# The next segment's features made between the matmuls of the last queries, in a segmented-attention and bilinear-GLU block on one core

## The chip, the cores and the metric

The kernel runs on one core of a Trainium2 chip. The core has five engines with a queue each, which run in order: PE (TensorE, matrix products and transposes into the accumulation memory PSUM), ACT (ScalarE), DVE (VectorE), POOL (GpSimd) and SP, which only issues DMAs here (ACT issues some too). The metric is the device time of one execution in microseconds; lower is better. The kernel before takes 881.73 us (median of three runs, 881.40 to 882.42).

## The reference

One transformer block on x of 2048 rows and 512 columns. A vector c gives six modulation vectors (silu(c) @ w_mod). First half: normalise the rows, scale and shift them, and attend with 32 heads of width 16 in four segments of 512 rows:

```python
h = _layernorm(x) * (1 + ca) + sa
q, k, v = h @ wq, h @ wk, h @ wv            # heads of 16, four segments of 512 rows
for s in range(4):
    p = softmax(qs @ ks.T * scale + mask)   # mask adds -1e9 above the diagonal
    a_dot = p @ vs
    pq = phi(qs)                            # phi(t) = t + 1 if t > 0 else exp(t)
    a_mem = (pq @ M) / (pq @ z + 1e-6)      # memory of the segments before
    o = g * a_mem + (1 - g) * a_dot         # g = sigmoid(beta), one per head
    pk = phi(ks)
    M, z = M + pk.T @ vs, z + pk.sum()
x = x + ga * (o @ wo)
```

Second half: normalise again, then ((h @ w_gate) * (h @ w_up)) @ w_down, and add gb times that to x.

## The kernel before

A segment's normalised rows are kept turned around, as *features*: for each 128 of the 512 columns d a tile of 128 x 512 (columns by rows), split in a high part ahH_d (rounded to the fast float32 format) and a low part ahL_d, the rest. A product is then three matmuls per d: high x high, low x high, high x low. The text calls these three matmuls a *triple*.

The attention half is one long loop (the last in the part shown). Its step v handles four heads of one segment (eight steps a segment, 32 in all; a place is written (v, slot)), and has five slots. In each slot PE first runs a **q step** (logits with queries in the rows, whose maximum DVE takes from PSUM: tiles q, nm), then in slot 1 the **tb** products (attention weights times v), then *fill*, and at the end a **k step** (logits with keys in the rows, out of which ACT makes the exponentials, tile pt, and POOL sets the part beyond the diagonal to zero). Each k step needs the exponential of the k step before to have emptied its PSUM tile (lk has one buffer), and a q step needs DVE to be done with the last one.

The **fill** is all the other PE work, in generators that hand out one piece at a time (fill_a, line 955; fill, line 1044). A slot has a credit; a triple costs 0.68 of it, a feature 0.45, a row step nothing. If a generator yields False, the fill of this slot stops there and the credit stays. For each segment s and each group g of eight heads the fill computes kps and qps (a_kq, line 747: k and q of the group, four triples each, over d = 0 to 3), splits them in three bfloat16 parts on ACT and POOL and writes them to DRAM; in the first group also v (vps). Between come the memory steps (mp, up, mz, mT: tiles in the one PSUM buffer sm, emptied by ACT as pkr and us).

The features of the next segment come from ln (line 207) with pfx "a", as a generator a_ln of 13 steps. Nine are *row steps*: four statistics (bn_stats), one for the row scale (ACT and POOL), four that normalise a tile of 128 rows in place (TENSOR_SCALAR x). Four are *feature steps*, one per d: four transposes on PE into a PSUM bank (atp_d), then ACT scales and shifts out of PSUM (ahf, line 205) and rounds to the high part (ahH, line 222), then POOL subtracts for the low part (ahL, line 223). There are eight feature tiles, one set: the next segment's ahH_d goes where this segment's lies, so it can be written only when the last qps (group 3) has read it. The PSUM banks of features, kps, qps and vps are two buffers of tag ms (bank, line 110).

weave(a, b, at) (line 669) hands out a, and after a's i-th piece that costs anything takes as many pieces of b as i stands in at; a False of b is passed on. In the kernel before, lines 977 to 980 weave the nine row steps into groups 2 and 3, and the four feature steps are what is left: they run behind the last qps (line 963), with a False after every second one (line 230).

DVE, ACT and POOL instructions follow the order in which the code and a scheduler put them; row steps are pinned behind the matmul that precedes them in the program.

Of the kernel before, what the change touches and what calls it, by code (L numbers as in the profile page):

```python
# [58 lines left out]
def tile_kernel(ctx, tc, x, wq, wk_, wv, wo, beta, w_gate, w_up, w_down, c, w_mod, out):  # L59
# [147 lines left out]
    def ln(pool, hpool, xt, s, sc, sh, pfx, hb, fast, kept_h=None):  # L207

        first = pfx == "a" and s == 0
        V, A = (CV, CA) if first else (vec, act)  # L210
        yield from ln_rows(pool, xt, s, pfx)
        hH, hL = [], []
        for d in range(KT):
            h = pool.tile([P, L], F32, tag="hf", name=f"{pfx}hf{s}_{d}", bufs=hb[2])
            ln_col(bank(f"{pfx}tp{s}_{d}"), h, xt, d, sc, sh, A)
            hi = hpool.tile([P, L], F32R, tag=hb[0].format(d), name=f"{pfx}hH{s}_{d}", bufs=hb[1])
            lo = hpool.tile([P, L], F32R, tag=hb[0].format(4 + d), name=f"{pfx}hL{s}_{d}", bufs=hb[1])
            if fast:
                V.tensor_copy(hi, h)
                V.tensor_sub(lo, h, hi.bitcast(F32))  # L220
            else:
                act.activation(hi, h, AF.Copy)
                nc.gpsimd.tensor_sub(lo, h, hi.bitcast(F32))  # L223
            hH.append(hi)
            hL.append(lo)
            if kept_h is not None:
                kept_h.append(h)
            yield 0.45
            if not first and d % 2 == 1:
                yield False  # L230
        return hH, hL

# [436 lines left out]
    def weave(a, b, at):  # L669

        i = 0
        for w in a:
            yield w
            if w:
                for _ in range(at.count(i)):
                    w = next(b, None)
                    if w or w is False:
                        yield w
                i += 1
# [275 lines left out]
    def fill_a():  # L955
        for w in w2:
            next(w)
        yield from av
        memq.extend((a_mem(0, 0), a_mem(0, 1)))
        lns = None  # L960
        for s in range(NSEG):
            if s > 0:
                hcur[0] = yield from lns
                if s < 3:
                    r = load_mod(2 * s)
            for g in range(2 if s == 0 else 0, NG):
                ws = []
                if s == 0 and g < 3:
                    ws = [load_g(nm, w, g + 1) for nm, w in (("k", wk_), ("q", wq))]
                for w in ws:  # L970
                    next(w)
                K, Q = a_kq(s, g, "k"), a_kq(s, g, "q")
                if g >= 2 and s + 1 < NSEG:
                    if g == 2:
                        xts[s + 1] = xload(s + 1)
                        lns = a_ln(s + 1)
                        Q = weave(Q, lns, (0, 1, 2, 3) if s > 0 else (2, 3))
                    else:
                        K = weave(K, lns, (0, 2) if s > 0 else (0, 1, 2, 3))
                        Q = weave(Q, lns, (0, 1, 2))  # L980
                if g == 1 and 0 < s < 3:
                    acc = mod_acc(r)
                    K, Q = weave(K, acc, (0, 2)), weave(Q, acc, (0, 2))
                if s == NSEG - 1 and g == 1:
                    xr0 = xr_load(0, pa, (0, 1), "x")
                    ready = chain(wo_weights(), wo_op(0, None, B["orl"], us[0]))
                if s == NSEG - 1 and 0 < g < NG - 1:
                    K, Q = weave(K, ready, (0, 1, 2, 3)), weave(Q, ready, (0, 1, 2, 3))
                if s == NSEG - 1 and g == NG - 1:
                    yield from weave(Q, ready, (0, 1, 2, 3))  # L990
                    memq.append(a_mem(s, g))
                    yield from K
                    yield from ready
                    yield from wo_mm(0, us[0], xr0, (0, 1))
                    break
                yield from K
                for w in ws:
                    next(w)
                yield from Q
                if s > 0 and g == 0:  # L1000
                    while vfree[0] < s:
                        yield None
                    if s < 3:
                        yield from weave(a_v(s), mod_acc(r), (1, 3, 5, 7))
                        yield from a_mod(2 * s, r[0])
                        r = load_mod(2 * s + 1)
                    else:
                        yield from a_v(s)
                        B["orl"] = wo_load(0, wpool)
                if g == 1 and 0 < s < 3:  # L1010
                    yield from a_mod(2 * s + 1, r[0])
                memq.append(a_mem(s, g))
        while memq or memt:
            yield mem_step() or 0.0
            yield False
# [283 lines left out]
    for q in range(2):  # L1299
# [98 lines left out]
        for m in range(2):  # L1398
            s = 2 * q + m
# [111 lines left out]
```

## Time and profile before

| | |
|---|---|
| runs | 882.42, 881.73, 881.40 us |
| the profiled execution | 881.91 us, its span 879.8 us |
| mean granted PE clock | 0.992 |
| PE busy | 832.8 us (95% of the span) |
| DVE, ACT, POOL busy | 650.6, 472.5, 424.1 us |

The profile shows one execution. The timeline has a row for each instruction or run of equal ones: start, length, engine, line, operation, tiles (output<-inputs), size, count, and in brackets how long the engine sat idle before it and what ended that. Most helpers record at line 90 (matmuls), 93 (transposes) or 40 (DVE in the loop), so instructions are told apart by tiles. Matmuls overlap: one of 512 columns is listed with 0.39 us, but the next starts 0.23 us later. The sums by stretch give, for each stretch, its length and then the busy time (and the number of instructions) of PE, PE's weight loads, DVE, ACT and POOL, then the granted PE clock, the busy share of the DMA engines and GB/s; for PE alone they give the length, PE, the clock and the DMA columns. The chain that ended last gives time slices: start, length, what.

### The profile page before, as it was taken

The page shows a single profiled execution, that of the slowest core. Times are in us where ns is not written, and L with a number is a line of the kernel's source. Part 1 is how long each engine was busy: PE and PEld are TensorE (multiplying, and loading weights), DVE is VectorE, ACT ScalarE, POOL GpSimd, SP SyncE. Part 2 cuts the span into 40 slices and gives each one's busy share as a digit, 9 for nine tenths or more (in the row PEclk, how much of TensorE's full clock was granted, in tenths as well). Part 3 has the DMA queues.
Part 4 walks back from the last instruction along what each step waited for, and adds up shares of the span by engine and source line. Part 5 has one row for each costly group of instructions (what it writes and reads, how often), then busy time and mean ns, then how long its engine had stood idle before and what let it go on. Part 6 is the DMA issues. An engine that isn't in the chain of part 4 may idle for free.

```text
span 879.8 us, 14406 instructions
## 1 busy us (share of the span) xinstructions
PE 832.8 (95%) x4824; PEld 583.0 (66%) x4824; DVE 650.6 (74%) x1728; ACT 472.5 (54%) x740; POOL 424.1 (48%) x564
## 2 busy tenths in 40 slices
PE   8998999989999989999978899999999999999998
PEld 5765565555565656655644567788778888887886
DVE  7697677986778868788888759898784856666532
ACT  3757667777677766777554664333363523333321
POOL 4545546546455665486352533987200846550000
PEclk9999899999999999999999999999999999999999
DMA  7774456665648665677695552543414232212032
GB/s 236 225 235 159 146 160 201 214 209 174 207 142 252 199 190 157 220 234 239 209 285 177 160 180 97 176 146 105 163 30 127 87 120 64 56 55 93 0 118 96
DMA packets 112667, 139.46 MB, mean 159 GB/s; under 512 B 20112, under 2 KB 71312, under 8 KB 112592
## 3 DMA queue, kind: packets, MB, share of 16 engines
q1 hardware_dynamic: 106368, 130.91, 48.7%
q10 hardware_dynamic: 6224, 7.62, 2.4%
q8 instruction: 38, 0.62, 0.3%
q14 instruction: 37, 0.30, 0.1%
HBM read 87.48 MB, written 50.76 MB: 157 GB/s over the span
## 4 chain that ended last, share of the span: by engine, by line
PE 66%; DVE 13%; DMA 8%; ACT 5%; POOL 4%; issue 3%; ACTq 1%; SPq 0%; POOLq 0%; DVEq 0%
PE g L90 23%; PE acc L90 14%; PE tb L90 5%; DVE q L40 5%; PE k L90 5%; PE q L90 5%; PE vps L90 4%; PE kps L90 3%; PE qps L90 2%; ACT pt L330 2%; DMA xr<-in_x_dram 2%; PE wops L90 2%; POOL ahL L223 1%; DVE x L40 1%; DVE nm L40 1%
## 5 line engine op out<-in xcount | busy, mean ns | idle before, releaser
L40 DVE CUSTOM_DVE_ANT_0 q<-q,cmask 128x384 f32<-128x384 f32 (+3 forms) x512 | 246.7, 508 | 66.4 <-PE q L90 56.4
L330 ACT ACTIVATE pt<-k 128x1024 f32<-128x1024 f32 x160 | 163.8, 1024 | 68.7 <-PE k L90 47.3
L333 POOL TENSOR_SCALAR_AFFINE_SELECT pt<-pt 128x256 f32<-128x256 f32 (+1 forms) x224 | 105.4, 484 | 174.3 <-ACT pt L330 173.9
L90 PE MATMUL q<-kst,qst 96*128 96x384 bf16 (+3 forms) x512 | 102.1, 301 | 11.7 <-DVE nm L40 10.4
L90 PE MATMUL k<-qst,kst 98*128 98x384 bf16 (+3 forms) x512 | 97.9, 303 | 11.6 <-ACT pt L330 10.7
L448 POOL TENSOR_TENSOR w<-w 128x256 f32<-128x256 f32 (+1 forms) x84 | 72.0, 869 | 55.7 <-DMA w<-in_w_up_dram 38.2
L443 POOL TENSOR_TENSOR AL<-w,AH 128x512 fp32r<-128x512 f32 (+1 forms) x42 | 58.2, 1388 | 48.0 <-ACT AH L439 46.8
L90 PE MATMUL tb<-pt,v 128*32 128x512 f32 (+3 forms) x1024 | 76.2, 438 | 0.2 <-POOL pt L333 0.2
L90 PEld LDWEIGHTS <-kst 98*128 98x128 bf16 x512 | 38.8, 99 | 56.6 <-issue 48.4
L40 DVE DVE_READ_ACCUMULATOR2_ANT nm<- 128x1 f32 x512 | 72.3, 141 | 0.0
L90 PEld LDWEIGHTS <-qst 96*128 96x128 bf16 x512 | 43.6, 98 | 39.1 <-issue 14.4
L439 ACT ACTIVATE AH<-w 128x512 fp32r<-128x512 f32 (+3 forms) x88 | 46.8, 565 | 33.6 <-POOL w L448 20.5
L1453 DVE TENSOR_TENSOR mL<-mid,mH 128x512 fp32r<-128x512 f32 (+1 forms) x44 | 32.9, 751 | 41.4 <-ACT mH L1452 39.4
L90 PE MATMUL acc<-DH,mL 128*128 128x512 f32 x144 | 56.6, 393 | 0.9 <-DVE mL L1453 0.9
L90 PE MATMUL acc<-DH,mH 128*128 128x512 f32 x144 | 57.2, 397 | 0.0
L90 PE MATMUL acc<-DL,mH 128*128 128x512 f32 x144 | 56.5, 393 | 0.0
L90 PEld LDWEIGHTS tb<-pt,v 128*32 128x32 f32 x1024 | 28.7, 110 | 39.5 <-issue 35.9
L1452 ACT ACTIVATE mH<-mid 128x512 fp32r<-128x512 f32 (+1 forms) x44 | 27.1, 627 | 51.7 <-PE acc L90 50.1
L1245 ACT ACTIVATE p<-g 128x512 f32<-128x512 f32 (+1 forms) x22 | 13.1, 597 | 73.2 <-PE g L90 73.1
L443 DVE TENSOR_TENSOR AL<-w,AH 128x512 fp32r<-128x512 f32 (+3 forms) x44 | 29.2, 671 | 19.1 <-ACT AH L439 18.2
L359 ACT ACTIVATE tsb<-tb 128x512 f32<-128x512 f32 x32 | 19.1, 596 | 35.0 <-PE tb L90 33.4
L90 PE MATMUL g<-chH,AH 128*128 128x512 f32 (+1 forms) x88 | 34.8, 395 | 0.7 <-ACT p L1245 0.7
(286 smaller groups left out, 2060.1 us busy)
## 6 DMA issues: line engine op xcount, KB each, us to landing
kst<-kd SPq DMA_DIRECT2D x32, 384.0 KB
qst<-qd SPq DMA_DIRECT2D x32, 384.0 KB
td<-tsb ACTq DMA_DIRECT2D x28, 256.0 KB
wm<-in_w_mod_dram SPq DMA_DIRECT2D x24, 256.0 KB
kd<-k SPq DMA_DIRECT2D x16, 384.0 KB
qd<-q SPq DMA_DIRECT2D x16, 384.0 KB
w<-in_w_gate_dram SPq DMA_DIRECT2D x40, 128.0 KB
w<-in_w_up_dram SPq DMA_DIRECT2D x40, 128.0 KB
```

Of the source, the lines that this page charges most:

```text
L40: i = getattr(self.eng, name)(*a, **k)
L90: return pe(nc.tensor.matmul(*a, **k))
L223: nc.gpsimd.tensor_sub(lo, h, hi.bitcast(F32))
L330: lpt[0] = act.activation(pt, kp, AF.Exp, scale=0.25)
L333: sels[u, i] = nc.gpsimd.affine_select(w, w, pattern=[[0, w.shape[1]], [1, P]], compare_op=ALU.is_ge, fill=0.0, base=0, channel_multiplier=-1)
L359: act.activation(tsbs[u], tbs.pop(u), AF.Copy)
L439: i = act.activation(hi[sl], w[sl], AF.Copy)
L443: i = eng.tensor_sub(lo[sl], w[sl], hi[sl].bitcast(F32))
L448: i = ce.tensor_tensor(w[:, o, :, 0:n], w[:, x, :, 0:n], w[:, y, :, 0:n], op=op)
L1245: lcp[0] = act.activation(r["p1"], ps, AF.Copy)
L1452: pin(act.activation(mH[0:n], md[0:n], AF.Copy))
L1453: vec.tensor_sub(mL[0:n], md[0:n], mH[0:n].bitcast(F32))
```

## The change

It concerns the steps of a_ln alone. The False after every second feature is kept only for the second normalisation (pfx "c"). The four feature steps of the next segment are woven into Q of group 3, one behind each of its triples, so that feature d is written where the triple before it has just read. The row steps start one piece sooner (behind the last piece of K of group 2, or, in segment 0, behind the first of Q instead of the third) and all nine are handed out by the end of K of group 3.

```diff
@@ -226,7 +226,7 @@
             if kept_h is not None:
                 kept_h.append(h)
             yield 0.45
-            if not first and d % 2 == 1:
+            if pfx == "c" and d % 2 == 1:
                 yield False
         return hH, hL
 
@@ -974,10 +974,12 @@
                     if g == 2:
                         xts[s + 1] = xload(s + 1)
                         lns = a_ln(s + 1)
-                        Q = weave(Q, lns, (0, 1, 2, 3) if s > 0 else (2, 3))
+                        if s > 0:
+                            K = weave(K, lns, (3,))
+                        Q = weave(Q, lns, (0, 1, 2, 3))
                     else:
-                        K = weave(K, lns, (0, 2) if s > 0 else (0, 1, 2, 3))
-                        Q = weave(Q, lns, (0, 1, 2))
+                        K = weave(K, lns, (0, 1, 2, 3) if s > 0 else (0, 1, 1, 2, 3))
+                        Q = weave(Q, lns, (0, 1, 2, 3))
                 if g == 1 and 0 < s < 3:
                     acc = mod_acc(r)
                     K, Q = weave(K, acc, (0, 2)), weave(Q, acc, (0, 2))
```

How this moves instructions is seen in three places (the number at the end of a name only counts the tiles). PE before, in (1, 3), from segment 0 to 1: behind the q step stand two features in a row; the last qps has ended in slot 2.

```order
L90 MATMUL q_1_1_1098<-kst_227,qst_231 128x128
L93 MATMUL atp_0_1109<-ident,x_0_690 128x128
L93 MATMUL atp_0_1109<-ident,x_1_692 128x128
L93 MATMUL atp_0_1109<-ident,x_2_694 128x128
L93 MATMUL atp_0_1109<-ident,x_3_696 128x128
L93 MATMUL atp_1_1120<-ident,x_0_690 128x128
L93 MATMUL atp_1_1120<-ident,x_1_692 128x128
L93 MATMUL atp_1_1120<-ident,x_2_694 128x128
L93 MATMUL atp_1_1120<-ident,x_3_696 128x128
```

PE now, in (1, 2): the second feature between two triples of the last qps; ahH_1 and ahL_1, which it will overwrite, have just been read.

```order
L90 MATMUL qps_3_980<-ahH_1_425,wqH_687 128x512
L90 MATMUL qps_3_980<-ahH_1_425,wqL_688 128x512
L90 MATMUL qps_3_980<-ahL_1_426,wqH_687 128x512
L93 MATMUL atp_1_1078<-ident,x_0_690 128x128
L93 MATMUL atp_1_1078<-ident,x_1_692 128x128
L93 MATMUL atp_1_1078<-ident,x_2_694 128x128
L93 MATMUL atp_1_1078<-ident,x_3_696 128x128
L90 MATMUL qps_3_980<-ahH_2_442,wqH_687 128x512
L90 MATMUL qps_3_980<-ahH_2_442,wqL_688 128x512
L90 MATMUL qps_3_980<-ahL_2_443,wqH_687 128x512
```

In all three hand-overs the features' transposes move in this way: from two slots of two features each to one feature in a slot, or two in one slot and none in the next, with triples between them, and the next segment's kps starts one or two slots sooner.

POOL before, at the same hand-over (AFFINE_SELECT sets the part beyond the diagonal to zero; kr, qr and the k or q lines are the bfloat16 splits): the four low halves stand close together, behind the first split of the last q.

```order
L333 AFFINE_SELECT pt_2_1081<-pt_2_1081 128x2x128 x2
L771 TENSOR_TENSOR qr_3_1075<-qf_3_1072,q_0_3_1074 128x512
L333 AFFINE_SELECT pt_3_1135<-pt_3_1135 128x2x128 x2
L223 TENSOR_TENSOR ahL_0_1116<-ahf_0_1108,ahH_0_1115 128x512
L780 TENSOR_TENSOR q_0_3_1074<-qr_3_1075,q_0_3_1074 128x512
L223 TENSOR_TENSOR ahL_1_1127<-ahf_1_1119,ahH_1_1126 128x512
L333 AFFINE_SELECT pt_4_1172<-pt_4_1172 128x4x128
L223 TENSOR_TENSOR ahL_2_1153<-ahf_2_1145,ahH_2_1152 128x512
L223 TENSOR_TENSOR ahL_3_1164<-ahf_3_1156,ahH_3_1163 128x512
```

POOL now: they are spread from pt_0 to pt_4, three of them ahead of the last q's splits.

```order
L223 TENSOR_TENSOR ahL_0_1017<-ahf_0_1009,ahH_0_1016 128x512
L333 AFFINE_SELECT pt_1_1059<-pt_1_1059 128x2x128
L223 TENSOR_TENSOR ahL_1_1085<-ahf_1_1077,ahH_1_1084 128x512
L333 AFFINE_SELECT pt_2_1096<-pt_2_1096 128x2x128 x2
L333 AFFINE_SELECT pt_3_1139<-pt_3_1139 128x2x128 x2
L223 TENSOR_TENSOR ahL_2_1124<-ahf_2_1116,ahH_2_1123 128x512
L771 TENSOR_TENSOR qr_3_1133<-qf_3_1130,q_0_3_1132 128x512
L333 AFFINE_SELECT pt_4_1187<-pt_4_1187 128x4x128
L223 TENSOR_TENSOR ahL_3_1159<-ahf_3_1151,ahH_3_1158 128x512
L780 TENSOR_TENSOR q_0_3_1132<-qr_3_1133,q_0_3_1132 128x512
```

ACT now, in the second hand-over (slots (8, 2) to (8, 4)): four of the rows are feature work (ahf, ahH), which before stood behind all of the rows here, beyond the tb of (9, 1).

```order
L802 ACTIVATE phk_3_2347<-kf_3_2345 128x512
L205 ACTIVATE ahf_0_2365<-atp_0_2366,modc 128x512
L330 ACTIVATE pt_2_2381<-k_2_2376 128x1024
L310 DMA qst_229<-nt_2387 1x16x128
L779 CAST k_1_3_2347<-kr_3_2348 128x512
L222 ACTIVATE ahH_0_2372<-ahf_0_2365 128x512
L310 DMA qst_229<-nt_2387 1x16x128
L205 ACTIVATE ahf_1_2405<-atp_1_2406,modc 128x512
L330 ACTIVATE pt_3_2421<-k_3_2416 128x1024
L222 ACTIVATE ahH_1_2412<-ahf_1_2405 128x512
```

ACT before, at the same place, without them.

```order
L802 ACTIVATE phk_3_2347<-kf_3_2343 128x512
L330 ACTIVATE pt_2_2371<-k_2_2366 128x1024
L310 DMA qst_229<-nt_2377 1x16x128
L779 CAST k_1_3_2345<-kr_3_2346 128x512
L310 DMA qst_229<-nt_2377 1x16x128
L765 ACTIVATE qf_3_2400<-qps_3_2358 128x512
L850 ACTIVATE pkr_2_2411<-mp_2_2406 128x512
L770 ACTIVATE q_1_3_2402<-qf_3_2400 128x512
L330 ACTIVATE pt_3_2418<-k_3_2413 128x1024
```

Each exponential (pt) now waits for the feature work ahead of it, and with it the k step behind.

## The prediction

> **What bounds the kernel now.** First the page: span, and the chain that ended last.
>
> ```profile
> span 879.8 us, 14406 instructions
> ...
> PE 66%; DVE 13%; DMA 8%; ACT 5%; POOL 4%; issue 3%; ACTq 1%; SPq 0%; POOLq 0%; DVEq 0%
> ```
>
> TensorE carries two thirds of the chain; the question is where in the loop it waits. So second the sums by stretch: lines 1, 3 and 5 are the three hand-overs from one segment to the next (from the last q matmuls of segment s to the first k and q matmuls of s+1), the others are plain loop.
>
> ```profile
> 74.15:96.66 22.51, 19.86 (x136) 10.96 (x136) 12.93 (x50) 14.90 (x23) 11.78 (x15) 0.85 0.51 166
> 104.04:177.03 72.99, 71.47 (x526) 44.06 (x525) 60.43 (x215) 52.89 (x79) 41.23 (x62) 1.00 0.63 192
> 177.03:210.35 33.32, 28.72 (x207) 17.64 (x203) 24.76 (x86) 25.54 (x39) 19.44 (x26) 1.00 0.61 190
> 210.35:273.92 63.57, 61.68 (x436) 38.85 (x433) 50.09 (x176) 44.96 (x65) 34.15 (x51) 1.00 0.62 188
> 296.15:326.02 29.87, 25.06 (x191) 15.71 (x190) 23.39 (x78) 22.08 (x34) 19.84 (x26) 1.00 0.62 190
> 326.02:358.16 32.14, 32.08 (x227) 20.28 (x224) 24.13 (x91) 20.15 (x28) 14.28 (x24) 1.00 0.59 186
> ```
>
> The first numbers are length and PE busy. In the plain stretches PE fills 97 to 99.8%; in the hand-overs it fails to by 2.7, 4.6 and 4.8 us, and in the first its clock was 0.85. Third, the chain through the end of the second hand-over:
>
> ```profile
> 195.01 0.87 PE atp L93 x8
> 195.89 0.44 PE k L90 x4
> 196.33 0.17 PE ntp L93
> ...
> 198.77 2.92 POOL ahL L223 x2
> ...
> 202.41 1.24 POOL ahL L223
> 203.66 0.04 issue
> 203.70 0.50 PE kps L90
> ...
> 204.66 0.44 PE q L90 x4
> ...
> 205.85 1.40 PE qps L90 x6
> ...
> 208.13 2.29 PE tb L90 x32
> ```
>
> All four features are made in a lump, and POOL's low halves (ahL, 1.24 us each) then stand between TensorE and the first kps. The same rows price PE's work: a step of q or of k 0.44, a triple of kps or qps 1.40 / 2 = 0.70, one feature's transposes 0.87 / 2 = 0.435 (I take the same for mp and mT, four transposes each), ntp 0.17, tb 2.29, a handed-over wait 0.04.
>
> **The clock.** In the first hand-over the lump costs more:
>
> ```profile
> 84.20:87.60 3.40, 1.67 (x8) 1.00 0.91 306
> 87.60:91.00 3.40, 3.00 (x6) 0.50 0.92 276
> 91.00:94.40 3.40, 3.40 (x16) 0.50 0.29 99
> ...
> 200.00:203.40 3.40, 1.93 (x6) 1.00 0.74 240
> ...
> 483.50:486.96 3.46, 1.83 (x12) 1.00 0.07 24
> 486.96:490.40 3.44, 3.44 (x14) 0.50 0.70 203
> ```
>
> After 1.67 and 1.83 us of PE work in 3.4 us the clock fell to half; after 1.93 us it held. At half clock 3.00 + 3.40 us of work cost 3.2 us extra. The Trainium skill (TensorE: Matmul & The Clock Gate, HAM oscillation) says that the gate drops after matmul gaps of more than about 3.4 us; by that rule neither this stretch nor the changed one would lose its clock, and the sum would stay as it is below. The trace disagrees: the longest wait near the first fall is the 1.29 us of the next row, so the measured windows decide.
>
> ```profile
> 87.82 0.80 PE L90 MATMUL kps<-ahL,wkH 128*128 128x512 f32 x1 [1.29 <-POOL ahL L223]
> ```
>
> **The change, part by part.** No instruction is added or removed. Four things move. (1) The feature steps stand between qps triples of group 3, not behind them. (2) The stops (False) go, so the fill no longer breaks off after two features. (3) Row steps (statistics, normalising) come one to three slots sooner. (4) On SP the load of the next w_mod rows passes the last qd writes in the first two hand-overs, on POOL and ACT the last q split goes behind features. From v = 20, slot 4 on, the PE order is the same, so the sum is over three hand-overs.
>
> Prices of the memory steps inside, and the ACT and DVE prices:
>
> ```profile
> 302.62 0.73 PE L90 MATMUL up<-MZ,phq 128*128 128x136 f32 x4 [1.03 <-ACT pkr L850]
> 303.19 0.60 PE L90 MATMUL k<-qst,kst 98*128 98x256 bf16 x4
> ...
> 305.24 1.19 PE L90 MATMUL mz<-v,pkr 128*128 128x136 f32 x8 [0.49 <-ACT us L867]
> 306.26 0.60 PE L90 MATMUL k<-qst,kst 98*128 98x512 bf16 x2
> ```
>
> up takes 0.57, mz 1.02 (start to next start).
>
> ```profile
> 180.52 0.61 ACT L802 ACTIVATE phk<-kf 128x512 f32<-128x512 f32 x1
> 181.04 1.00 ACT L330 ACTIVATE pt<-k 128x1024 f32<-128x1024 f32 x1
> 181.94 0.60 ACT L779 CAST k<-kr 128x512 bf16<-128x512 f32 x1
> ...
> 188.56 1.02 ACT L330 ACTIVATE pt<-k 128x1024 f32<-128x1024 f32 x1 [1.72 <-PE k L90]
> ...
> 195.58 1.45 ACT L205 ACTIVATE ahf<-atp,modc 128x512 f32<-128x512 f32 x2
> ```
>
> ACT moves on after 0.52 for a copy, 0.90 for an exponential, about 0.7 for a feature out of PSUM.
>
> I walk each engine's new order from a point that both orders share, each piece starting when its engine and its inputs are ready.
>
> First hand-over, from the tb at 74.15 to the k step before at 96.66. PE work now: 2 tb 4.58, 10 steps of q or k 4.40, 7 triples 4.90 (one more than before, since the first feature took a triple's place ahead of 74.15), 3 features 1.31, mp 0.44, ntp 0.17: 15.80. Waits: adding these pieces up from 74.15, the last feature's transposes end at 82.7 and its copy out of PSUM (behind an exponential, a high half and the q split) at 84.4; the k step two triples later ends at 84.5, its exponential, which ACT's order puts ahead of the last high half, at 85.4, the high half at 86.0, POOL's select and low half at 87.85. PE has a q step and five matmuls more until 86.1, and then waits 1.75. Together 17.55 against 22.51: **5.0 saved**, 3.2 of it clock. That tb stands where it stood: ahead of it DVE takes all four statistics sooner, two of them (1.62 us, first rows below) before a q step, and wins the time back where it waited 1.95 us for the row scale (third row). I take 0 for this; the ends are +1.6, nothing won back, and -0.4, one normalising step fewer before the last q.
>
> ```profile
> 59.12 0.69 DVE L40 BATCH_NORM_STATS2 ast<-x 128x6 f32<-128x512 f32 x1
> ...
> 60.74 0.41 DVE L40 CUSTOM_DVE_ANT_0 q<-q,cmask 128x256 f32<-128x256 f32 x1
> ...
> 71.41 0.55 DVE L40 TENSOR_SCALAR x<-x,amv,ay 128x512 f32<-128x512 f32 x1 [1.95 <-POOL ay L191]
> ```
>
> Second, 177.03 to 210.35, same work in both: 20 steps 8.80, 11 triples 7.70, 4 features 1.74, mp and mT 0.87, 2 ntp 0.34, 2 up 1.14, mz 1.02, 2 tb 4.58: 26.2. Waits, with ACT busy without a pause from 178.8 to 192.5 because the features stand ahead of its exponentials (its 1.72 us pause at 188.56 goes): from phk at 180.52 its order runs first feature 181.0, exponential 181.7, copy, high half, second feature 183.7, exponential 184.35, high half, third feature 185.8, qf, pkr 187.0 to 187.55, high half, exponential 188.0, q split, us 189.4 to 189.8, fourth feature, high half, second us, exponential 191.5. PE would start the first up at 186.45 and waits for pkr 1.1; it would start the second at 188.5 and waits for us 1.35; k steps wait for an exponential 0.15 and, behind the tb at 193.6, 0.6; others 0.4: 3.6. 33.3 - 29.8 = **3.5 saved**.
>
> Third, 296.15 to 326.02: 18 steps 7.92, 9 triples 6.30, 4 features 1.74, mp and mT 0.87, 2 ntp 0.34, 2 up 1.14, mz 1.02, 2 tb 4.58: 23.9. Waits, by the same walk: first feature at 299.3 on ACT, copy, high half, exponential 301.0 to 302.0, where PE is ready for its k step at 301.05: 0.95; the fourth feature's bank is emptied 0.35 late; the second up and mz wait for the two us, behind two features and two exponentials, 0.35 and 0.75: 2.4. 29.87 - 26.3 = 3.55, and one qps triple more (0.70) is then done: **4.25 saved**.
>
> Ten handed-over waits at 0.04 to 0.06 take 0.5 back. Net 12.2. What stands at nothing: the row steps in the second and third (+0.9 for a statistics pair at each if PE did not cover them; there PE fills 71.47 of 72.99); the reordered memory steps in 210 to 274 (PE is short of full by 1.89 there: from -1.9 to +1.9); the SP shifts (those q rows are loaded ten or more us later); the fall at 487, whose window may slide off its waits when all comes earlier (-1.7 or 0). The profiled run took 881.91 (span 879.8), 0.18 above the median of 881.73: 881.91 - 12.2 = 869.7, so 869.5 as a median.
>
> **The rivals.**
> - The clock falls anyway. In the changed first hand-over the window 84.2 to 87.6 still holds 1.5 of the 1.75 us wait: 1.9 us of work, between 1.83 (fell) and 1.93 (held). If it falls, 3.2 come back: 872.7.
> - Slower: one PSUM bank for the features. qps keeps one of the two banks of tag ms, so each feature waits until ACT has emptied the other. If every feature finds an exponential and two copies ahead of its own (0.90 + 2 x 0.52 + 0.7 = 2.64) while PE has only a triple, a q and a k step (1.58) to do, it stalls 1.06, and 12 features cost 12.7: the whole gain. It decides from about 1.1 us per feature beyond my walk; at 1.3, 3 us slower: 884.7. Against it: the walk finds the bank empty in time except once (0.35).
> - Nothing: the fill is held by its credit or by the gate on v tiles, and the time moves to later slots: 881.7. Against it: PE is not short of work in the hand-overs, it waits.
> - DVE and POOL get in each other's way. Two normalising steps took 1.00 beside little, 2.00 beside POOL's subtraction:
>
> ```profile
> 179.25 1.00 DVE L40 TENSOR_SCALAR x<-x,amv,ay 128x512 f32<-128x512 f32 x2
> ...
> 184.47 2.00 DVE L40 TENSOR_SCALAR x<-x,amv,ay 128x512 f32<-128x512 f32 x2
> ```
>
>  If half of the 12 x 1.24 us of ahL holds up a DVE that PE waits for, 7.4 come back: 877. The Trainium skill (SBUF — State Buffer, Who interferes with whom) has such instructions exclude each other; the doubled row agrees. Against the rival: DVE's idle time grows where PE's waits go.
>
> **How the numbers follow.** Forecast (clock kept, walk right within 4) 0.55; clock falls 0.19; DVE against POOL 0.08; better than 864 0.05; nothing 0.05; slower 0.08. Low end: half of the 7.75 us of waits also vanish (3.9) and the fall at 487 goes (1.7): 869.5 - 5.6 = 864. High end: clock 3.2, statistics 1.6, memory steps 1.9: 876.2. Within 0.2% (1.8 us, about what runs of this kernel can tell apart) is same. Faster 0.55 + 0.19 + 0.08 + 0.05 = 0.87.
>
> **What would show it.** Right: the three hand-overs shorter by about 5, 3.5 and 4; the granted clock at 1.00 in the first; waits of kps for ahL nearly gone, except one of 1 to 2 us in the first; new waits of k steps for pt and of up for us; the same times from one k step to the next after v = 24. Wrong: waits of atp for ahf above 1 us, DVE steps of double length in the hand-overs, or plain stretches that grow by what the hand-overs lose.

## The result and the profile after

The changed kernel takes 893.4 us (median of four runs, 892.15 to 894.91) and the kernel before 881.57 (four runs, 880.21 to 882.42) beside it: a ratio of 1.0136, 95% interval 1.0114 to 1.0159. It is 12 us slower; 869.5 us was forecast. Ratios here and below count runs in the usual clock state alone; three later runs were slower (895 us in e7_wo_mod, 930 and 1027 us in e14_sooner_phi, whose median is 880.3 us without them). The profiled execution took 894.91 us, 13.0 more than that of before. First the page of the changed kernel: span and the chain that ended last.

```profile
span 893.0 us, 14432 instructions
...
PE 65%; DVE 11%; DMA 9%; ACT 7%; POOL 3%; issue 3%; ACTq 1%; SPq 1%; POOLq 0%; DVEq 0%
```

Then what PE waited for in the attention loop: total, times, longest. Before:

```profile
PE k L90 <- ACT pt L330: 10.7, 11, 2.3
PE q L90 <- DVE nm L40: 10.4, 24, 0.9
PE kps L90 <- POOL ahL L223: 4.3, 7, 1.3
```

and after:

```profile
PE q L90 <- DVE nm L40: 18.6, 25, 3.9
PE k L90 <- ACT pt L330: 12.9, 12, 1.9
PE up L90 <- ACT us L867: 3.7, 4, 1.2
...
PE atp L93 <- DVE x L40: 1.6, 1, 1.6
...
PE kps L90 <- POOL ahL L223: 1.1, 1, 1.1
```

The wait at which the change aims (kps for ahL) fell from 4.3 to 1.1 us. But q steps now wait 8.2 us more for DVE's maxima (nm), with nearly the same number of waits: a few have become long. The sums by stretch tell where. They run between the same steps as the rows in the prediction (length, busy time of PE, PE's weight loads, DVE, ACT and POOL, granted clock, DMA):

```profile
75.02:93.66 18.64, 16.93 (x136) 9.70 (x136) 12.39 (x47) 13.97 (x22) 11.87 (x16) 1.00 0.64 201
101.58:183.51 81.93, 74.33 (x527) 44.69 (x525) 61.59 (x221) 52.82 (x79) 39.94 (x62) 0.96 0.59 179
183.51:214.01 30.50, 28.15 (x208) 17.68 (x204) 23.11 (x78) 25.19 (x39) 19.57 (x26) 0.99 0.56 177
214.01:281.46 67.45, 62.76 (x436) 39.44 (x433) 49.72 (x176) 44.71 (x65) 34.04 (x51) 0.97 0.60 188
305.52:334.72 29.20, 25.77 (x194) 16.04 (x194) 24.30 (x76) 22.73 (x35) 21.06 (x27) 1.00 0.51 158
367.20:417.77 50.57, 44.97 (x303) 27.28 (x301) 39.21 (x135) 34.43 (x53) 33.77 (x42) 0.97 0.71 220
```

Lines 1, 3 and 5 are the hand-overs: 18.64, 30.50 and 29.20 us where they took 22.51, 33.32 and 29.87. They did become shorter, by 3.9, 2.8 and 0.7. The plain stretches lost more: line 2 takes 81.93 for 72.99 (+8.9), line 4 67.45 for 63.57 (+3.9), and the last, from (20, 4) to (24, 0), 50.57 for 45.15 (+5.4), whose row of before is

```profile
358.16:403.31 45.15, 43.31 (x303) 26.95 (x301) 38.45 (x132) 34.07 (x51) 33.06 (x42) 1.00 0.71 223
```

In these three the granted clock is below 1.00 too, where it was 1.00 before. 2.4 us of line 2 seem to be chance: at (6, 4) two small DMAs that ACT issues (qst<-nt) started 2.7 us behind the start of the exponential ahead of them, and the next exponential and a k step of PE (1.86 us) waited. In e1_late_norm, whose code is the same up to there, they started 0.6 us behind it and no time was lost; what held them is not shown.

The largest loss sits in (8, 1), just ahead of the second hand-over. The chain of waits through it:

```profile
171.84 0.19 ACT asd L181
172.04 0.06 issue
172.10 1.17 POOL qr L771
173.27 0.59 POOL pt L333
173.86 0.17 POOL aya L187
...
174.12 0.20 POOL ayb L189
174.31 1.11 POOL q L780
175.42 0.16 POOL ayb L190
175.58 0.36 POOL pt L333
175.94 0.18 POOL ay L191
176.11 0.03 issue
176.14 0.03 DVE x L40
176.17 0.43 issue
176.60 0.56 DVE q L40
```

and the two rows of the timeline that belong to it, DVE's and PE's:

```profile
176.14 0.55 DVE L40 TENSOR_SCALAR x<-x,amv,ay 128x512 f32<-128x512 f32 x1 [4.44 <-POOL ay L191]
...
177.66 0.59 PE L90 MATMUL q<-kst,qst 96*128 96x256 bf16 x2 [3.93 <-DVE nm L40]
```

The row scale (ay) is 0.2 us steps on ACT and POOL, each behind whatever else those queues hold: a split of q (1.17 and 1.11 us), selects of pt. From the last statistics to the finished scale it takes 5.7 us (170.40 to 176.11). The first normalising step now follows the scale by one triple, so DVE stood 4.44 us in front of it, with the next q step's maxima behind it, and PE with them (3.93 us, and 0.32 more in the same q step). The clock then fell to half, and (8, 1) took 10.6 us for 3.8. In the kernel before the same step came at 179.25 (a row in the prediction), 2.3 us behind the finished scale (176.97), without a wait; now DVE comes to it 1.3 us behind the last statistics.

### The profile page after: what moved, and what is told of

Read it like the earlier page. It is cut to its first block, busy times and chain, and to the rows that moved or that the text cites. A ratio compares the mean times of both kernels' runs of the same rounds, so it can differ in the third digit from the quotient of the medians.

```text
span 893.0 us, 14432 instructions
## 1 busy us (share of the span) xinstructions
PE 837.8 (94%) x4823; PEld 585.8 (66%) x4824; DVE 653.7 (73%) x1728; ACT 472.1 (53%) x740; POOL 420.6 (47%) x564
## 4 chain that ended last, share of the span: by engine, by line
PE 65%; DVE 11%; DMA 9%; ACT 7%; POOL 3%; issue 3%; ACTq 1%; SPq 1%; POOLq 0%; DVEq 0%
PE g L90 23%; PE acc L90 14%; PE tb L90 6%; PE k L90 5%; DVE q L40 5%; PE q L90 4%; PE vps L90 3%; PE kps L90 3%; PE wops L90 2%; ACT pt L330 2%; PE qps L90 2%; PE mz L90 1%; DMA orl<-od 1%; DMA wor<-in_wo_dram 1%; DMA x<-in_x_dram 1%
## 5 line engine op out<-in xcount | busy, mean ns | idle before, releaser
L333 POOL TENSOR_SCALAR_AFFINE_SELECT pt<-pt 128x256 f32<-128x256 f32 (+1 forms) x224 | 103.5, 476 | 185.5 <-ACT pt L330 183.2
L90 PE MATMUL tb<-pt,v 128*32 128x512 f32 (+3 forms) x1024 | 80.0, 456 | 0.0
```

What stands on the lines that cost most here:

```text
L90: return pe(nc.tensor.matmul(*a, **k))
L333: sels[u, i] = nc.gpsimd.affine_select(w, w, pattern=[[0, w.shape[1]], [1, P]], compare_op=ALU.is_ge, fill=0.0, base=0, channel_multiplier=-1)
```

## The experiments

Theory Q, formed from these rows: the features' move does what was forecast, and the time is lost where an in-order queue holds a moved step ahead of its input. Its rivals are in the expectations: F, that the features between the triples cost the time themselves; B, that a wait taken away comes back at the next place. They were run on two chips, the last three on one and the others on the other, beside runs of before that spread from 877 to 889 us around medians of 881.5 to 882.3, so ratios and stretches of the trace count more than single times. The table in this section has the stretches.

**Each part by itself.** e1_late_norm, in the changed kernel:

```diff
-                        K = weave(K, lns, (0, 1, 2, 3) if s > 0 else (0, 1, 1, 2, 3))
+                        K = weave(K, lns, (1, 2, 3, 3) if s > 0 else (0, 1, 1, 2, 3))
```

> The changed kernel with its first normalising step one triple later in the second and third hand-over (K of group 3 takes the row steps at 1, 2, 3, 3 and not at 0, 1, 2, 3); PE's order stays the same, on DVE the first TENSOR_SCALAR x passes one q step. Theory Q (queues: the hand-overs became shorter, and the time went at three places outside the forecast, where an in-order queue holds a moved step ahead of its input; at (8, 1) that step is the normalising one, which waits 4.44 us for the row scale with the q step behind it): the 4.25 us wait of PE in (8, 1) shrinks to 0 to 2 and the clock does not fall at 177, together 5 to 7 of the 6.8 us lost there: 893.4 - 6 = 887 (885.5 to 889). Theory F (the features between the triples cost the time, by PSUM banks, by ACT or by DVE and POOL in each other's way): no gain there, 892 to 895.

Measured: 887.2 us, ratio 1.0049 (1.0019 to 1.0078). (8, 1) is back at 3.3 us. As theory Q said, one step put one triple later is worth more than half of the loss (0.0087 in the ratio, 7.7 us; 7.3 us in the trace at this place). But DVE still waits for the scale, a q step later (so (8, 2) waits now, 1.6 us), and the clock still fell, at 176 us, which theory Q had excluded: the rows (8, 1) to (10, 0) together are only 4.9 us shorter than in the changed kernel.

```profile
173.17 0.55 DVE L40 TENSOR_SCALAR x<-x,amv,ay 128x512 f32<-128x512 f32 x1 [2.17 <-POOL ay L191]
```

e2_rows_only, the changed kernel with features and stops put back:

```diff
-            if pfx == "c" and d % 2 == 1:
+            if not first and d % 2 == 1:
...
                         K = weave(K, lns, (0, 1, 2, 3) if s > 0 else (0, 1, 1, 2, 3))
-                        Q = weave(Q, lns, (0, 1, 2, 3))
```

> Row steps as in the changed kernel; the four feature steps stay behind the last qps in a lump, with the stops, as before. Theory Q: the wait for the row scale stands in (8, 1) as in the changed kernel (about 6.8 us with the clock), the first hand-over loses up to 1.5 more, and no hand-over gains, except what a longer lead of the statistics is worth: 881.6 + 7 = 888.5 (886 to 891). Theory F: nothing is lost without the features' move, 880 to 883.

Measured: 889.54, ratio 1.0074 (1.0054 to 1.0095), with the same wait of DVE at the same place and no feature moved:

```profile
175.74 0.55 DVE L40 TENSOR_SCALAR x<-x,amv,ay 128x512 f32<-128x512 f32 x1 [4.42 <-POOL ay L191]
```

That settles this part: the row steps alone make the kernel about 7 us slower.

e3_feat_only, the changed kernel with the row steps of before as far as the features allow:

```diff
-                        if s > 0:
-                            K = weave(K, lns, (3,))
-                        Q = weave(Q, lns, (0, 1, 2, 3))
+                        Q = weave(Q, lns, (0, 1, 2, 3) if s > 0 else (2, 3))
...
-                        K = weave(K, lns, (0, 1, 2, 3) if s > 0 else (0, 1, 1, 2, 3))
+                        K = weave(K, lns, (0, 2, 3, 3, 3) if s > 0 else (0, 1, 2, 3, 3, 3, 3))
```

> Features between the triples and no stops, as in the changed kernel; the statistics and the row scale stand where they stood before, and the rest of the row steps is handed out by the end of K of group 3 (at its last pieces), since the features need it. Theory Q: the hand-overs keep their gain (about 8 to 9 in all), the 6.8 us at (8, 1) are not lost; the other two places, (11, 1) and (22, 0) to (22, 1), some 4.5 and 6 us, depend on how the later fill falls on the slots and may stay: 873 without them, 885 with both, I take 880. Several normalising steps in one slot may cost 1 us in the first hand-over. Theory F: 890 to 895, since the features stand where they stand in the changed kernel.

Measured: 893.14, ratio 1.0114 (1.0074 to 1.0154). A miss for theory Q's 880: with the normalising steps at the end of K the features themselves wait for x in all three hand-overs,

```profile
PE atp L93 <- DVE x L40: 5.7, 6, 1.8
```

so the features cannot move without the row steps. The time lies in F's range (890 to 895), so it does not tell the theories apart. The trace doesn't speak for F's bank or ACT: features wait for DVE's x. But two of the steps they wait for ran 1.37 and 1.44 us, where most take 0.54, beside a subtraction on POOL, which is the third part of F.

e4_stops_only, in the kernel before:

```diff
-            if not first and d % 2 == 1:
+            if pfx == "c" and d % 2 == 1:
```

> The kernel before without the stops after every second feature (the one line at 229), nothing else. Theory Q: the lump is made in fewer slots, the later fill moves against the slots by a piece or two; if that shift alone brings the waits at (11, 1) or (22, 0), 885 to 888, else 880.5 to 883. Theory F: the lump is tighter, so the features wait more for ACT: 882 to 885.

Measured: 880.49, ratio 0.9974 (0.9947 to 1.0001). Without the stops the kernel is no slower and perhaps 2 us faster (the interval reaches 1); F's 882 to 885 didn't come. None of the waits at (11, 1) and (22, 0) is in its trace.

**The other two places.** In the changed kernel (11, 1) and (22, 0) to (22, 1) hold the next long waits. The rows of DVE and PE at the first (before, the same step of DVE did not wait; it is the row on top), and at the second POOL's row of before, then the chain of waits in the changed kernel:

```profile
220.44 1.47 DVE L40 SCALAR_TENSOR_TENSOR phq<-phq,rlq 128x512 f32<-128x512 f32 x1
...
223.64 0.69 DVE L40 SCALAR_TENSOR_TENSOR phq<-phq,rlq 128x512 f32<-128x512 f32 x1 [2.48 <-ACT phq L802]
...
226.34 0.38 PE L90 MATMUL q<-kst,qst 96*128 96x256 bf16 x2 [2.56 <-DVE nm L40]
```

```profile
370.19 2.54 POOL L931 TENSOR_TENSOR wor<-wor,gab 128x512 f32<-128x512 f32 x2
...
374.10 8.69 DMA wor<-in_wo_dram
382.79 0.07 issue
382.86 1.29 POOL wor L931
384.15 0.02 issue
384.18 0.63 ACT woH L935
384.81 0.91 ACT pt L330
385.72 0.53 ACT woH L935
386.25 0.02 issue
386.27 0.03 DVE woL L40
```

At the first, DVE's phi step of q (the minimum with 1 and the sum, line 814, handed out behind the next q step) has come one q step ahead of where it was, while ACT's exponential for it (222.97) stands behind two w_mod rows, a split of q, a v and two exponentials of pt (218.92 to 222.97). At the second, POOL scales rows of wo that have not landed, ACT rounds what POOL has not scaled, DVE subtracts what ACT has not rounded, and the exponential of pt and the maxima stand behind them. The load itself is late: SP issues it behind the write of a memory step (mTs, at 367.23; 354.01 in the kernel before), and that step's transposes moved from (20, 1) to (20, 3). The next edits are on top of e1_late_norm.

e5_wo_later:

```diff
-        for f, k in ((None, 0), (scaled, 0), (halves, 0),
+        for f, k in ((None, 0), (None, 0), (None, 0), (None, 0), (scaled, 0), (halves, 0),
```

> The kernel of e1_late_norm, and in wo_weights four empty pieces between the loads of wo and the first scaling of them on POOL, so that POOL, ACT and DVE (wor, woH, woL) come to them some four triples later. Theory Q (at (22, 0) and (22, 1) POOL waits 3.4 us for the wo rows, ACT for POOL, DVE for ACT, with the exponential and the q step behind them): the waits of PE there (1.7 for pt, 2.7 for nm in e1_late_norm) and the fall of clock at that place go, 5 to 7 us less than e1_late_norm: 881 (879.5 to 882.5). Theory B (DMA bandwidth in that stretch, or the later fill as a whole, costs the time and the waits only move): within 1.5 of e1_late_norm, 886 to 889.

Measured: 888.32, ratio 1.007 (1.0039 to 1.0101), no better than e1_late_norm. In its trace (22, 1) took 5.7 us less, but (23, 0) and (23, 1) 3.8 more, where POOL now waits for the second pair of rows:

```profile
390.04 1.29 POOL L931 TENSOR_TENSOR wor<-wor,gab 128x512 f32<-128x512 f32 x1 [2.13 <-DMA wor<-in_wo_dram]
```

So B was right for this edit: the wait moved on.

e6_mod_later:

```diff
-                        yield from weave(a_v(s), mod_acc(r), (1, 3, 5, 7))
+                        yield from weave(a_v(s), mod_acc(r), (5, 7, 9, 11))
```

> The kernel of e1_late_norm, and the scaling of w_mod rows on ACT (wm) taken between later pieces of v (5, 7, 9, 11, not 1, 3, 5, 7): at (11, 1) two wm rows of 0.72 then stand behind phq on ACT instead of ahead of it. Theory Q (at (11, 1) DVE's pinned phq step waits 2.48 us for ACT's phq with two q steps behind it): the wait shrinks by the 1.3 of two wm rows, and the clock, which fell at 228, may hold (1.5 more): 2 to 3 less than e1_late_norm, 884.5 (883 to 886). Theory B: nothing, 886 to 889.

Measured: 888.69, ratio 1.0075 (1.0047 to 1.0103). The wait at (11, 1) shrank from 3.09 us in e1_late_norm to 2.43 only, and no gain can be seen in the time. e7_wo_mod has both edits.

> Both edits, of e5_wo_later and e6_mod_later, in the kernel of e1_late_norm. Theory Q: the three places add up, 6 + 2.5 less than e1_late_norm: 878.5 (876.5 to 880.5), faster than before by the gain of the hand-overs less what waits in (15, 3), (16, 3) and (19, 1). Theory B: 884 to 889.

Measured: 886.32, ratio 1.0045 (1.0015 to 1.0076): far from 878.5, within B's range. The two edits hit the neighbours of the causes, as e11_wo_two and e14_sooner_phi show below.

**Each hand-over by itself.** e8_first_only makes the change in the first hand-over and keeps the row steps, lump and stops of before in the others. In the kernel before:

```diff
-            if not first and d % 2 == 1:
+            if not first and (pfx == "c" or s > 1) and d % 2 == 1:
...
-                        Q = weave(Q, lns, (0, 1, 2, 3) if s > 0 else (2, 3))
+                        Q = weave(Q, lns, (0, 1, 2, 3))
...
-                        K = weave(K, lns, (0, 2) if s > 0 else (0, 1, 2, 3))
-                        Q = weave(Q, lns, (0, 1, 2))
+                        K = weave(K, lns, (0, 2) if s > 0 else (0, 1, 1, 2, 3))
+                        Q = weave(Q, lns, (0, 1, 2) if s > 0 else (0, 1, 2, 3))
```

> The kernel before with the change in the first hand-over alone (segment 0 to 1); the second and third keep their lump and its stops. Theory Q: the gain of the first hand-over in the trace of the changed kernel, 2.5 us (3.4 in e1_late_norm), is kept to the end, since the later fill falls on the slots as before: 879 (877.5 to 880.5) on runs of before at 882. Theory B: the gain is given back later, 881 to 883.

Measured: 880.2, ratio 0.9971 (0.9939 to 1.0003), in theory Q's range, though the interval just includes no gain, and the stops alone gave as much (e4_stops_only). e9_first_two changes the first two (with e1_late_norm's list), e10_third_only the third; in group 3 they have

```diff
+                        K = weave(K, lns, ((0, 1, 1, 2, 3), (1, 2, 3, 3), (0, 2))[s])
+                        Q = weave(Q, lns, (0, 1, 2, 3) if s < 2 else (0, 1, 2))
```

and

```diff
+                        K = weave(K, lns, ((0, 1, 2, 3), (0, 2), (1, 2, 3, 3))[s])
+                        Q = weave(Q, lns, (0, 1, 2, 3) if s == 2 else (0, 1, 2))
```

with the lists of group 2 and the stops to match.

> The change (with the later normalising step of e1_late_norm) in the first and second hand-over; the third keeps its lump and its stops. Theory Q, now with each loss tied to the hand-over that brings it (weaving delays the end of the last qps by four features, and with it the memory steps of that group, which then fall on the slots of the next segment's v): first hand-over -3, second -1 net of the wait in (8, 2), then +3 to +4.5 at (11, 1); nothing at (16, 3) and at (22, 1). Together 0, 881 to 883 on runs of before at 881.6. Rival S (any shift of the fill, from wherever, brings the waits at (22, 0) to (22, 1)): 886 to 889.

> The change (row steps as in e1_late_norm) in the third hand-over alone, the first two as before. Theory Q: nothing at (8, 1) and (11, 1); +2 to +3 at (16, 3), where the first feature waits for the last normalising step, -3 to -3.5 in the hand-over, +1.3 at (19, 1), +6 to +7 at (22, 0) to (22, 1), -1.3 at (23, 1): +5 to +6, 887 (885.5 to 888.5). Rival S: the waits at (22, 0) to (22, 1) come only when the first two are shifted as well, 880 to 883.

Measured: 883.88, ratio 1.0026 (0.9997 to 1.0055), and 883.31, ratio 1.0014 (0.9988 to 1.0039). (11, 1) waits 3.09 us in e9_first_two and (22, 1) doesn't; in e10_third_only it is the other way round, 2.92 us in (22, 1), so rival S is out. The median of e10_third_only is below what was expected, though its profiled run (885.98) showed every wait that was. By the ratios the first hand-over's change gives about 2.5 us, the second's costs 5 and the third's 1; with the 7 us of (8, 1) that makes 10.5 of the 12, and each ratio leaves 2 or 3 us open, so this is a rough account.

e11_wo_two, on e1_late_norm again, leaves the wo steps more room behind both loads:

```diff
-        for f, k in ((None, 0), (scaled, 0), (halves, 0), (scaled, 1), (halves, 1), (raw_load, 2), (raw_load, 3),
+        for f, k in ((None, 0),) + ((None, 3),) * 6 + ((scaled, 0), (halves, 0), (scaled, 1), (halves, 1), (raw_load, 2), (raw_load, 3)) + ((None, 3),) * 4 + (
```

> The kernel of e1_late_norm with empty pieces behind both pairs of wo loads, six behind the first and four behind the second (e5_wo_later had three, behind the first only; its wait moved to the second pair, (23, 0) and (23, 1), where POOL waited 2.13 us for the rows). Theory Q: both waits go, and the 5.75 us that e5_wo_later won at (22, 1) stay won: in the trace from (21, 4) to (24, 0) 5 to 7 us shorter than e1_late_norm, 882 (880 to 884). Theory B: the time comes back at the next wait, 886 to 889.

Measured: 886.43, ratio 1.0042 (1.0015 to 1.007). In its trace the waits at both loads are gone and (21, 0) to (23, 4) take 39.9 us for 46.3, but the median is only 0.8 below that of e1_late_norm, in B's range (886 to 889). This stayed inconclusive until e15_sooner_phi_wo. e12_first_nostop joins the two harmless halves; in e8_first_only:

```diff
-            if not first and (pfx == "c" or s > 1) and d % 2 == 1:
+            if pfx == "c" and d % 2 == 1:
```

> A version meant to beat both: the change in the first hand-over (e8_first_only), and no stops in the other two lumps (e4_stops_only). Theory Q: the 2.5 to 3 us of the first hand-over stay; the lumps without stops gave between -1 and +1 each: 879.5 (877.5 to 881) on runs of before at 881.6. Theory B: 881 to 883.

Measured: 880.83, ratio 0.9968 (0.9943 to 0.9994): a little faster than before.

**The causes one after another.** The last three take the changed kernel, with PE's order untouched, and give each late input its time. e13_rows_sooner:

```diff
-                            K = weave(K, lns, (3,))
-                        Q = weave(Q, lns, (0, 1, 2, 3))
+                            K = weave(K, lns, (3, 3))
+                        Q = weave(Q, lns, (0, 0, 1) if s > 0 else (0, 1, 2, 3))
...
-                        K = weave(K, lns, (0, 1, 2, 3) if s > 0 else (0, 1, 1, 2, 3))
+                        K = weave(K, lns, (0, 1, 1, 2) if s > 0 else (0, 1, 1, 2, 3))
```

> The changed kernel with the row steps of the second and third hand-over sooner still: two statistics behind the last piece of K of group 2, two behind the first of Q, the row scale behind the second (two triples sooner than in the changed kernel), and the normalising steps at 0, 1, 1, 2 of K of group 3. PE's order is that of the changed kernel. Theory Q (DVE waits in (8, 1) because the row scale comes last): the wait in (8, 1) goes, 6.8 us; the second hand-over keeps its 3 us; the 1.6 us for x in (16, 3) goes; pairs of statistics may cost 0.5 each: 8 less than the changed kernel, +4 on before, ratio 1.0045 (1.002 to 1.007). Theory F (features): ratio 1.012 to 1.015.

Measured: 885.77, ratio 1.0034 (1.0012 to 1.0056), as theory Q said. The scale is ready at 163.49 and DVE comes to the first normalising step at 170.05, without a wait. The scale itself took 1.7 us from the last statistics (161.80), not 5.7: handed out sooner, its steps on POOL no longer stand behind the splits of q.

```profile
163.29 0.20 POOL L191 TENSOR_TENSOR ay<-ay,ayb 128x4 f32<-128x4 f32 x1
```

```profile
170.05 0.55 DVE L40 TENSOR_SCALAR x<-x,amv,ay 128x512 f32<-128x512 f32 x1
```

The features stand where they stand in the changed kernel, and 9 of the 12 us are back (1.0136 to 1.0034): F is out as the main cause. e14_sooner_phi adds, for the first group of a segment (flush, line 742, now takes each step once, and that step puts itself back once):

```diff
-                later.append(lambda: pin(vec.scalar_tensor_tensor(e, e, 1.0, rl, op0=ALU.min, op1=ALU.add)))
+                step = lambda: pin(vec.scalar_tensor_tensor(e, e, 1.0, rl, op0=ALU.min, op1=ALU.add))
+                later.append((lambda: later.append(step)) if s > 0 and g == 0 and nm == "q" else step)
```

> The kernel of e13_rows_sooner, and the phi step of q (phq on DVE) of a segment's first group held back by one slot, behind the next q step. PE's order stays. Theory Q: at (11, 1) the 3.09 us wait and the fall of clock go, and the 1.09 at (19, 1): (10, 1) to (11, 4) take 25 us, not 28.5; together 4 less than e13_rows_sooner, ratio 1.000 (0.997 to 1.003). Theory A (ACT is overloaded there, and whoever comes next waits): at most 1 less.

Measured: 880.5, ratio 0.9973 (0.9945 to 1.0000). PE has no wait left at (11, 1), where e13_rows_sooner still waited:

```profile
219.15 0.38 PE L90 MATMUL q<-kst,qst 96*128 96x256 bf16 x2 [2.56 <-DVE nm L40]
```

The 1.09 us at (19, 1) went too: there it was the same step of the next segment. ACT's load is as it was, so theory A is out (at most 1 us was its forecast; it is 5): what counts is where DVE's step stands. e15_sooner_phi_wo adds the edit of e11_wo_two.

> The kernel of e14_sooner_phi, and the empty pieces behind both pairs of wo loads of e11_wo_two. Theory Q: (21, 0) to (23, 4) take 40, not 45 us; of the 5 to 6 some 1.5 come back as DVE's later steps for orl at (25, 0): 4 less than e14_sooner_phi, ratio 0.9955 (0.992 to 0.998), faster than before by what the three hand-overs and the memory steps win. Theory B (it comes back later in full): ratio of e14_sooner_phi within 0.0015.

Measured: 877.36, ratio 0.994 (0.9911 to 0.9968), 0.0033 below e14_sooner_phi on the same chip: the wo edit is worth some 3 us here, about half of the 6.3 us that (21, 0) to (23, 4) became shorter. A wait of 1.37 us of PE for DVE's orl at (25, 0) is new. On e1_late_norm the same edit gave 0.8 us, so its worth is known only roughly. This version is faster than both kernels. The stretches of the profiled runs, in us, from the end of one k step to that of another (the first from the start):

| stretch | before | changed | e1 later norm | e13 rows sooner | e14 + phi | e15 + wo |
|---|---|---|---|---|---|---|
| to (0, 4) | 69.7 | 71.2 | 69.1 | 69.4 | 70.7 | 70.7 |
| (1, 0) to (2, 2), hand-over | 29.5 | 25.5 | 26.6 | 28.2 | 26.6 | 28.2 |
| (2, 3) to (8, 0) | 74.7 | 77.1 | 74.7 | 75.3 | 76.0 | 76.2 |
| (8, 1) | 3.8 | 10.6 | 3.3 | 3.4 | 3.4 | 3.4 |
| (8, 2) to (10, 0), hand-over | 30.1 | 27.0 | 29.5 | 28.0 | 28.0 | 28.0 |
| (10, 1) to (11, 4) | 24.8 | 28.5 | 26.8 | 28.8 | 23.6 | 23.6 |
| (12, 0) to (15, 1) | 47.8 | 47.3 | 47.3 | 47.3 | 47.3 | 47.3 |
| (15, 2) to (16, 1) | 14.6 | 17.2 | 15.7 | 17.0 | 17.0 | 17.0 |
| (16, 2) to (18, 1), hand-over | 31.7 | 31.0 | 32.1 | 29.1 | 29.1 | 29.1 |
| (18, 2) to (20, 4) | 33.8 | 34.3 | 34.3 | 34.3 | 32.9 | 32.9 |
| (21, 0) to (23, 4) | 40.1 | 45.2 | 46.3 | 45.7 | 46.3 | 40.0 |
| (24, 0) to (31, 4) | 116.2 | 114.8 | 116.3 | 114.7 | 115.7 | 116.5 |

One edit changes one or two rows. What moves beside them, in the first, third and last rows, moves in kernels whose code is the same there; in the first hand-over it is the clock (25.5 us without a fall, 26.6 with one half-clock window, 28.2 with two; more below).

## Why the prediction was wrong

- **"No instruction is added or removed"; the hand-overs.** The mechanism held: kps hardly waits for ahL any more, and the one wait that was forecast for the first hand-over, 1.75 us, came as 1.15 for ahL and 0.56 for ahH. The sizes were too large: 3.9, 2.8 and 0.7 us against 5.0, 3.5 and 4.25. One error was in the sum: the unit prices gave 15.8, 26.2 and 23.9 us of PE work, and the rows above have 16.93, 28.15 and 25.77. The same prices put against the rows of before would have come out 2.5 us short in the second (26.2 for 28.72); a sum of prices was subtracted from a measured length. In the third, the first feature also waited 1.58 us for a normalising step, which the walk did not have. And the 3.2 us priced for the clock in the first were too much: in e10_third_only, whose code is that of before up to there, the clock held, and (1, 0) to (2, 2) took 28.3 us for 29.5.
- **"The row steps in the second and third" at nothing.** This step failed, by 6.8 us in the trace and about 7 in the medians (e1_late_norm, e2_rows_only). It was priced as work on DVE, 0.9 us for a pair of statistics, covered by PE. What counted was the distance from the row scale to the step that needs it. DVE's wait of 1.95 us for the same scale in the first hand-over was quoted in the prediction, as a place where time is won back; the same wait was not asked for where a step was moved closer to it.
- **"From v = 20, slot 4 on, the PE order is the same, so the sum is over three hand-overs".** This was false: mT, up and triples of kps and qps stand in other slots up to (23, 3). It hid the 5.1 us of (21, 0) to (23, 4). Weaving four features into the last q moves the end of that q, and with it the memory steps; for a whole segment SP's loads and DVE's steps then stand in another order around them.
- **"The reordered memory steps (from -1.9 to +1.9)".** The place was named and the bound was wrong: +3.6 us in (10, 1) to (11, 4). The bound came from the 1.89 us that PE was short of full there before the change; DVE's wait for the phi step alone was 2.48 us.
- **"The SP shifts" at nothing.** What cost time on SP was not the q rows that were looked at, but the wo rows, whose load went behind a later mTs.
- **The statistics ahead of the first hand-over, 0 with ends +1.6 and -0.4.** Within the ends: 71.2 us to (0, 4) for 69.7. Kernels without the sooner steps took 68.4 to 69.7 there, those with them 69.1 to 71.4.
- **The rivals.** Against the bank: features wait 0.3 us for ahf in all, so it is out. DVE against POOL: single doubled steps appear, as in the prediction, but none at the three places decides; one (1.00 us at 308.42, beside a split of k) is part of the 1.58 us in the third hand-over. The clock: in the changed kernel's profiled run it held in the first hand-over, as forecast, but that was luck. Twelve profiled kernels have the changed code up to there; in five the clock held, in seven it fell (e13_rows_sooner is one). The chance of 0.19 was too small, and the price of 3.2 us too high: a fall cost 1.1 us (five kernels) or 2.7 (two). The rival that came true was not on the list: a step moved closer to its input on a queue that others need. The chance of 0.08 for slower was much too small for a change that moves pinned steps on four queues.
- **What stays open.** (15, 2) to (16, 1) takes 2.6 us more in the changed kernel, 1.1 in e1_late_norm and 2.4 in the last three. In the first two the second up and mz wait 1.65 us for ACT's copies to the tile us (0.95 before), with the row scale's steps between them on ACT; the changed kernel has a half-clock window behind that, too. In the last three PE waits 1.4 us for the tile us and 1.2 for DVE's maxima. No run took that apart.

## What to carry to other kernels

When a step is moved on an in-order queue, look first at what it will wait for and who stands behind it: the distance in time from its input's last producer, through every queue on the way, decides, not its own length. Work that is moved between slots moves everything that is handed out behind it, so compare the orders of all engines to the end before calling a stretch unchanged. Where a wait has gone from a trace and the time has not, look for the next input that is late for the same reason, and compare stretches of several versions, not totals.

## What the hardware showed

The clock fell behind windows of 3.41 us that PE had filled to about a half or less, and in the rows below without a wait as long as the window. In the changed kernel (length, PE busy, granted clock, DMA):

```profile
153.29:156.70 3.41, 1.64 (x8) 1.00 0.57 207
156.70:160.11 3.41, 2.39 (x17) 1.00 0.47 143
...
224.97:228.38 3.41, 1.51 (x12) 1.00 0.83 287
228.38:231.80 3.42, 3.42 (x30) 0.50 0.07 25
289.82:293.23 3.41, 1.95 (x13) 1.00 0.52 178
293.23:296.65 3.42, 3.23 (x13) 0.50 0.56 155
```

All six rows lie on one grid of windows, 3.41 us apart. PE worked 1.64 us in the first and the clock held; it worked 1.95 us in the fifth and the clock fell. So the bound isn't one number of busy time in the trace, as the prediction had it (1.83 fell, 1.93 held); what decides stays open. The longest waits at the two falls are 2.56 and 0.85 us. The Trainium skill (TensorE: Matmul & The Clock Gate, HAM oscillation) ties the fall to gaps of more than about 3.4 us; these rows don't agree, and only the fall in (8, 1), behind a wait of 3.93 us, would be one by that rule. A half-clock window that PE fills costs about 1.7 us, half of its length. Two such windows follow the wait at (8, 1): of the 6.8 us there 4.25 are the wait, and most of the rest is the tb behind it, 4.50 us where it takes 2.36 at full clock (at 170.71 in e1_late_norm).

A load of wo rows, 256 KB, took 8.69 us from issue to landing (wor in the chain above), in a stretch in which the DMA engines were busy 0.71 of the time; in the kernel before, with the same share, the first two loads had landed when POOL came to them, 6.6 us behind the issue of the first, and it waited 0.29 us for the fourth.
